# Four-byte pairs for the on-chip transposes, B and C loaded ahead of x, and a reordered head, in a state-space-plus-FFN kernel

## The chip, the cores and the metric

The kernel runs on one core of one Trainium2 chip. The metric is the device time of one execution in microseconds (us). Most executions agree within 1%; a few were marked slow (more than 1.5% above the fastest of the same kernel) and are left out of ratios. "Before" and "after" are the kernels without and with the change. A run's name, such as e5, is that of an experiment below.

The engines are TensorE (PE in the profile; PEld is its weight load), VectorE (DVE), ScalarE (ACT), GpSimd (POOL) and SyncE (SP), which only issues loads and stores here.

## The reference

The first half is a chunked linear-attention recurrence over 4 batches, 8 heads, 768 tokens; the second half is a gated FFN on 3072 tokens.

```python
# x: (4, 8, 768, 32)  a: (4, 8, 768)  B, C: (4, 8, 768, 16), all float32
cum = cumsum(log(a)) per chunk of 32
y   = (C B^T * exp(cum_i - cum_j) * causal) x  +  exp(cum) * (C state)
state = exp(cum_last) * state + sum_j exp(cum_last - cum_j) * B_j x_j
# then, with y as (3072, 256), w_gate and w_val (256, 1536), w_out (1536, 256):
out = (relu(y w_gate) * (y w_val)) w_out
```

The kernel multiplies C by running products of a (the tile `FC`) and B by their reciprocals (`FB`), so that the decay is inside the operands.

## The kernel before: the parts that matter

The FFN runs in six blocks of 512 tokens. B and C must be scaled and turned (state index onto partitions) once per batch. Batch b+1 is prepared inside FFN block b, for b = 0, 1, 2; blocks 3 to 5 have nothing to prepare. Batch 0 is prepared in the head, before the first block. A preparation has three steps.

```python
def scale(j, b, t, eng):                 # step 1: f32 -> bf16, times FB or FC
    eng.tensor_tensor(
        out=sq[j, b][:, :, t * N:(t + 1) * N],
        in0=rows[j, b][:, t].rearrange("p (k n) -> p k n", n=N),
        in1=(FB if j == "B" else FC)[:, 2 * b + t].to_broadcast([128, K, N]), op=ALU.mult)

def turn(j, b):                          # step 2: 32 x 32 transposes on VectorE
    tq[j, b] = glob.tile([128, K, R], BF16, ...)
    nc.vector.transpose(tq[j, b], sq[j, b])

def tidy_b(b, r0, r1, eng):              # step 3: tokens back in order
    dst = BT[b][:, K * r0:K * r1].rearrange("p (r k) -> p r k", k=K)
    (eng.copy ...)(out=dst, in_=tq["B", b][:, :, r0:r1].rearrange("p k r -> p r k"))
# tidy_c: the same for C, times a mask, into two halves
```

Here K is 24 tokens per row, R is 32 rows and N is 16 state columns. A tidy reads bf16 elements that lie 64 bytes apart. The main loop:

```python
for b in range(NBLK):
    for n in (P + 1, P + 2):                     # x of the next two pairs of chunks
        if n < NPAIR: load_x(n, nc.sync)
    if b in (1, 2):                              # B and C of the next batch
        for j, src in (("B", B), ("C", C)):
            rows[j, b + 1] = load_rows(src, b + 1, nc.sync, ...)
    def prep(step):
        if step < 2:   scale("B", n, step, nc.gpsimd); scale("C", n, step, nc.gpsimd)
        elif step < 4: turn("BC"[step - 2], n)
        elif step < 8: # 8 of the 32 rows per step
            tidy_b(.., nc.scalar); tidy_c(.., 0, nc.scalar); tidy_c(.., 1, nc.gpsimd)
    ...                                          # four 256-wide FFN steps, twice
    for f in range(4, NF):                       # eight 512-wide FFN steps
        if b == 0 and f == 4:
            factors(2, 8)                        # FC of batches 1 to 3
            for n in range(1, NB): inverse(n)    # FB of batches 1 to 3
        gv(b, f)                                 # gate, val, relu, product h
        prep(f - 4)
        ...                                      # cast_x on GpSimd, state matmuls A_ps
    ...                                          # fout: the output matmuls o
in_order(tc)                                     # each engine keeps the order of the program
```

Of the kernel before, what the change touches and what calls it, by code (L numbers as in the profile page):

```python
# [7 lines left out]

FP32 = mybir.dt.float32
BF16 = mybir.dt.bfloat16  # L10
AF = mybir.ActivationFunctionType
ALU = mybir.AluOpType

# [16 lines left out]
def kernel(  # L30
# [27 lines left out]

    const = ctx.enter_context(tc.tile_pool(name="const", bufs=1))
    glob = ctx.enter_context(tc.tile_pool(name="glob", bufs=1))  # L60
    raw = ctx.enter_context(tc.tile_pool(name="raw", bufs=4))
    att = ctx.enter_context(tc.tile_pool(name="att", bufs=3))
    ffn = ctx.enter_context(tc.tile_pool(name="ffn", bufs=2))
    mm = ctx.enter_context(tc.tile_pool(name="mm", bufs=1, space=bass.MemoryType.PSUM))
# [9 lines left out]
    def load_rows(src, b, q, name):  # L74
        rows = glob.tile([128, 2, K * N], FP32, name="%s%d" % (name, b))
        q.dma_start(out=rows, in_=src[b].rearrange("(t q) (r k) n -> (q r) t (k n)", t=2, r=R))
        return rows

    def load_x(p, *qs):
        b, c0 = p // PPB, 2 * (p % PPB)  # L80
        xr = raw.tile([128, 2, NH, D], FP32, tag="xr", name="xr")
        for i in range(2):
            sl = slice((c0 + i) * 128, (c0 + i + 1) * 128)
            qs[i % len(qs)].dma_start(out=xr[:, i], in_=x[b, :, sl, :].rearrange("h s d -> s h d"))  # L84
        st[p] = {"xr": xr}
# [2 lines left out]
    av = a.rearrange("b (t q) (r k) -> (q r) (b t) k", t=2, r=R)  # L88
    nc.sync.dma_start(out=al[:, 0:2, 1:], in_=av[:, 0:2])
    rows = {}  # L90
    rows["B", 0] = load_rows(B, 0, nc.scalar, "br")
    rows["C", 0] = load_rows(C, 0, nc.sync, "cr")
    load_x(0, nc.sync, nc.scalar)
    nc.sync.dma_start(out=al[:, 2:, 1:], in_=av[:, 2:])

    first = const.tile([1, 2], FP32)
# [28 lines left out]
    def keep_warm(n):  # L125
        w = bank("w")
        for _ in range(n):
            nc.tensor.matmul(out=w, lhsT=warm[:, 0:128], rhs=warm, start=True, stop=True)

    keep_warm(8)  # L130

    wg = glob.tile([128, 2, DF], BF16)
    wv = glob.tile([128, 2, DF], BF16)
# [2 lines left out]
    def weights(f0, f1):  # L136
        fs = slice(f0 * 128, f1 * 128)
        for w, src in ((wg, moe_w_gate), (wv, moe_w_val)):
            nc.gpsimd.dma_start(
                out=w[:, :, fs], in_=src[:, fs].rearrange("(k p) f -> p k f", k=2))  # L140
# [8 lines left out]
    def wait_for(j, cell):  # L149
        nc.gpsimd.tensor_copy(gate[:, j:j + 1], cell)  # L150
# [24 lines left out]
    def inverse(b):  # L175
        nc.vector.reciprocal(FB[:, 2 * b:2 * b + 2], FC[:, 2 * b:2 * b + 2])
# [5 lines left out]
    CT = [glob.tile([128, 2, S], BF16, name="CT%d" % b) for b in range(NB)]  # L182


    sq, tq = {}, {}

    def scale(j, b, t, eng):
        if (j, b) not in sq:
            sq[j, b] = glob.tile([128, K, 2 * N], BF16, name="sq%s%d" % (j, b))
        eng.tensor_tensor(  # L190
            out=sq[j, b][:, :, t * N:(t + 1) * N],
            in0=rows[j, b][:, t].rearrange("p (k n) -> p k n", n=N),
            in1=(FB if j == "B" else FC)[:, 2 * b + t].to_broadcast([128, K, N]), op=ALU.mult)

    def turn(j, b):
        tq[j, b] = glob.tile([128, K, R], BF16, name="tq%s%d" % (j, b))
        nc.vector.transpose(tq[j, b], sq[j, b])  # L197

    def span(i, b, r0, r1):
        return tq[i, b][:, :, r0:r1].rearrange("p k r -> p r k")  # L200

    def tidy_b(b, r0, r1, eng):
        dst = BT[b][:, K * r0:K * r1].rearrange("p (r k) -> p r k", k=K)
        (eng.copy if eng is nc.scalar else eng.tensor_copy)(out=dst, in_=span("B", b, r0, r1))  # L204

    def tidy_c(b, t, r0, r1, eng):
        dst = CT[b][:, t, K * r0:K * r1].rearrange("p (r k) -> p r k", k=K)
        if eng is nc.scalar:
            eng.mul(dst, span("C", b, r0, r1), tmask[:, t:t + 1])  # L209
        else:  # L210
            eng.tensor_scalar_mul(dst, span("C", b, r0, r1), tmask[:, t:t + 1])  # L211

    yT = glob.tile([128, 2, T], BF16)
    A_ps = mm.tile([128, 2, 128], FP32, tag="Aps", name="A_ps")
# [60 lines left out]
    def astep(p, i):  # L275

        c = 2 * (p % PPB) + i
        if c == NC - 1:
            return
        nc.tensor.matmul(  # L280
            out=A_ps, lhsT=st[p]["B"][i], rhs=st[p]["x"][i],
            start=(c == 0), stop=(c == NC - 2), skip_group_check=True)

    def sevac(p, i):
        if 2 * (p % PPB) + i == NC - 1:
            return
        S[2 * p + i + 1] = n = att.tile([128, 2, 128], BF16, tag="Sm", name="Sm", bufs=5)
        nc.vector.tensor_tensor(out=n, in0=A_ps, in1=smask, op=ALU.mult)

    def state(p, i):  # L290
        astep(p, i)
        sevac(p, i)
# [98 lines left out]


    factors(0, 2)
    inverse(0)
    wait_for(0, al[0:1, 0, 1:2])
    weights(0, 4)
    scale("B", 0, 0, nc.vector)
    scale("C", 0, 0, nc.gpsimd)
    scale("B", 0, 1, nc.vector)
    scale("C", 0, 1, nc.vector)  # L400
    load_x(1, nc.sync)
    turn("B", 0)
    tidy_b(0, 0, 11, nc.scalar)
    turn("C", 0)
    tidy_c(0, 0, 0, 11, nc.scalar)
    tidy_c(0, 1, 0, 11, nc.vector)
    cast_x(0, nc.scalar)
    keep_warm(10)
    rows_b(0)
    G(0)  # L410
    astep(0, 0)
    sevac(0, 0)
    gevac(0, half=False)
    wait_for(1, st[1]["xr"][0:1, 1, 0, 0:1])
    weights(4, 8)
    load_x(2, nc.sync)
    rows["B", 1] = load_rows(B, 1, nc.sync, "br")
    rows["C", 1] = load_rows(C, 1, nc.sync, "cr")
    keep_warm(4)
    Dm(0)  # L420
    inter(0, 1)
    astep(0, 1)
    yevac(0, nc.scalar)
    tidy_b(0, 11, R, nc.scalar)
    tidy_c(0, 0, 11, R, nc.scalar)
    tidy_c(0, 1, 11, R, nc.gpsimd)
    rows_b(1)
    cast_x(1, nc.scalar)
    sevac(0, 1)

    for b in range(NBLK):
        P, Q, W = 2 * b + 2, 2 * b + 3, 2 * b + 1
        more = P < NPAIR
        for n in (P + 1, P + 2):
            if n < NPAIR:
                load_x(n, nc.sync)
        if b in (1, 2):
            for j, src in (("B", B), ("C", C)):
                rows[j, b + 1] = load_rows(src, b + 1, nc.sync, j.lower() + "r")

        def at(name, *fs):

            return more and f == fs[min(b, len(fs) - 1)]

        def prep(step):
            n = b + 1
            if n >= NB:
                return
            if step < 2:
                scale("B", n, step, nc.gpsimd)  # L450
                scale("C", n, step, nc.gpsimd)
            elif step < 4:
                turn("BC"[step - 2], n)
            elif step < 8:
                r = 8 * (step - 4)
                tidy_b(n, r, r + 8, nc.scalar)
                tidy_c(n, 0, r, r + 8, nc.scalar)
                tidy_c(n, 1, r, r + 8, nc.gpsimd)

        for f in range(4):  # L460
            gvh(b, f, 0)
            if b == 0 and f == 0:
                G(1)
                gevac(1)
                state(1, 0)
                weights(8, NF)
                wait_for(2, st[2]["xr"][0:1, 1, 0, 0:1])
                weights_out(0, NF)
            if f == (3 if b == 0 else 1):
                if b == 1:  # L470
                    state(W, 1)
                inter(W, 0)
                inter(W, 1)
                Dm(W)
                if b == 0:
                    state(1, 1)
                yevac(W, nc.scalar)
        for f in range(4):
            gvh(b, f, 1)
        for f in range(4, NF):  # L480
            if b == 0 and f == 4:
                factors(2, 8)
                for n in range(1, NB):
                    inverse(n)
            gv(b, f)
            if f in (4, 5):
                prep(f - 4)
            if f >= 6:
                prep(f - 4)
            if at("cast P", 6, 4, 4):  # L490
                cast_x(P, nc.gpsimd)
            if at("cast Q", 8, 5, 4):
                cast_x(Q, nc.gpsimd)
            if at("rows P", 7, 6, 5):
                rows_b(P)
            if at("state P0", 9, 8, 7):
                state(P, 0)
            if at("state P1", 10, 10, 9):
                state(P, 1)
            if at("rows Q", 99, 9, 8):  # L500
                rows_b(Q)
        if more:
            inter(P, 0)
            inter(P, 1)
        fout(b, 0)
        foevac(b, 0)
        if more:
            G(P)
            gevac(P)
        if b == 0:  # L510
            rows_b(Q)
        fout(b, 1)
        foevac(b, 1)
        if more and b > 0:
            state(Q, 0)
        fout(b, 2)
        foevac(b, 2)
        if more:
            Dm(P)
            yevac(P, nc.scalar)  # L520
            G(Q)
            gevac(Q)
            state(Q, 1 if b else 0)
        fout(b, 3)
        foevac(b, 3)
# [32 lines left out]
```

## Time and profile before

| | before |
|---|---|
| median of 3 runs | 150.23 us (149.98 to 150.93) |
| span of the profiled run | 147.2 us |
| head (to the first gate matmul of block 0) | 14.92 us |
| blocks 0, 1, 2 (start to start) | 25.56, 24.50, 26.24 us |
| blocks 3, 4 | 18.24, 18.12 us |
| block 5 with the last store | 19.62 us |
| mean granted TensorE clock | 0.954 |

A block starts here with its first `gv` matmul in the trace. Blocks 0 to 2 differ from 3 and 4 by about 6 to 8 us each, and the preparation is the work that only they have.

The table of stretches of before, from a block's start to its first output matmul (blocks 1, 2, 3); a row has the stretch, its length, busy time of each engine with the number of instructions, granted clock, DMA share, and GB/s:

```profile
core 0: us, PE busy (x) PEld busy (x) DVE busy (x) ACT busy (x) POOL busy (x), PEclk, DMA share, GB/s
...
40.48:57.06 16.58, 12.40 (x93) 7.48 (x92) 10.44 (x21) 10.33 (x23) 7.23 (x11) 0.98 0.41 95
...
64.98:83.06 18.08, 13.53 (x94) 7.69 (x93) 10.06 (x20) 10.18 (x23) 7.21 (x11) 0.91 0.38 88
...
91.22:102.79 11.57, 11.52 (x93) 7.22 (x92) 9.12 (x19) 9.20 (x20) 1.67 (x4) 1.00 0.37 70
```

In block 3 TensorE is busy for 11.52 of 11.57 us: it is the limit. In blocks 1 and 2 it does the same matmuls with gaps of 4.2 and 4.6 us, and no other engine is full. I read that as the latency of a chain, not a lack of rate; e1 and e8 bear it out. The timeline of block 1 of before shows the chain (start, duration, engine, line, operation, output and inputs, and in brackets how long the engine sat idle and what ended it; xN is the number of merged instructions):

```profile
41.77 2.83 SPq L84 DMA_DIRECT2D xr<-in_x_dram  x4
...
44.65 0.67 SPq L76 DMA_DIRECT2D br<-in_B_dram  x1
...
45.36 0.47 SPq L76 DMA_DIRECT2D cr<-in_C_dram  x1
...
48.95 0.84 POOL L190 TENSOR_TENSOR sqB<-br,FB 128x384 bf16<-128x384 f32 x1 [7.98 <-DMA br<-in_B_dram]
49.95 0.84 POOL L190 TENSOR_TENSOR sqC<-cr,FC 128x384 bf16<-128x384 f32 x1 [0.16 <-DMA cr<-in_C_dram]
50.73 0.61 POOL L219 CAST xb<-xr 128x512 bf16<-128x512 f32 x1
51.30 0.83 POOL L190 TENSOR_TENSOR sqB<-br,FB 128x384 bf16<-128x384 f32 x1
51.39 0.27 PE L280 MATMUL A_ps<-xb,bt 128*128 128x256 bf16 x1 [2.16 <-POOL xb L219]
...
52.17 0.98 DVE L197 STREAM_TRANSPOSE tqB<-sqB 128x768 bf16<-128x768 bf16 x1 [3.86 <-POOL sqB L190]
...
53.65 0.96 DVE L197 STREAM_TRANSPOSE tqC<-sqC 128x768 bf16<-128x768 bf16 x1
```

SyncE issues four x loads first, so B is issued 2.9 us after the queue is free. GpSimd waits 7.98 us for it. Because every engine keeps its order, the x cast stands behind the scales, TensorE's state matmul behind the cast, and VectorE's products behind the transpose.

The costs of the three steps, from the groups of before with shapes kept apart (line, engine, operation, count; total busy us, mean ns of one; idle before and what ended it):

```profile
L209 ACT ACTIVATE CT<-tqC,tmask 128x192 bf16<-128x192 bf16 x12 | 7.5, 626 | 2.8 <-DVE tqC L197 2.8
...
L204 ACT COPY BT<-tqB 128x192 bf16<-128x192 bf16 x12 | 6.2, 516 | 5.3 <-DVE tqB L197 5.3
...
L190 POOL TENSOR_TENSOR sqB<-br,FB 128x384 bf16<-128x384 f32 x6 | 5.0, 837 | 20.0 <-DMA br<-in_B_dram 15.5 <-DVE FB L176 4.5
...
L197 DVE STREAM_TRANSPOSE tqB<-sqB 128x768 bf16<-128x768 bf16 x4 | 3.9, 975 | 9.4 <-POOL sqB L190 9.4
...
L190 DVE TENSOR_TENSOR sqC<-cr,FC 128x384 bf16<-128x384 f32 x1 | 1.2, 1212 | 0.0
...
L190 DVE TENSOR_TENSOR sqB<-br,FB 128x384 bf16<-128x384 f32 x2 | 1.0, 554 | 0.0
```

The scales on VectorE are those of the head. Two took 0.55 us; the third ran beside a scale on GpSimd and took 1.21 us.

### The profile page before, as it was taken

To read this page: it belongs to the slowest core of one execution; us is meant where nothing else is said; L and a number is where in the kernel's file an instruction comes from. 1 tells how busy PE (TensorE), PEld (TensorE's weight loads), DVE (VectorE), ACT (ScalarE), POOL (GpSimd) and SP (SyncE) were. 2 spreads that over 40 slices of the span, in tenths; PEclk is the share of its full clock that TensorE was granted. 3 is DMA by queue.
4 is the path that set the end of the run, shared out by engine and by line. 5 is a ranking of instruction groups with operands and counts; after the bars stand their busy time and mean duration, and the time that the engine had idled before them with its cause. 6 is when DMAs were issued, how large, how long until landed. Compare 5 with 4: busy or idle time off the path is not lost.

```text
span 147.2 us, 2902 instructions
## 1 busy us (share of the span) xinstructions
PE 124.8 (85%) x1056; PEld 79.2 (54%) x1062; DVE 94.1 (64%) x201; ACT 89.2 (61%) x188; POOL 48.5 (33%) x78
## 2 busy tenths in 40 slices
PE   6945989677999459999709979999999999999991
PEld 2312564235785126677303557845777458774580
DVE  6964479975478185647607665778657786477711
ACT  4084856478588329568603975877359763687520
POOL 5509561975210668220155923010230102200000
PEclk9996599999999996899995999999999999999999
DMA  4999999900259200028900002640026000220022
GB/s 129 231 204 253 200 159 154 128 0 2 76 119 213 97 0 0 4 71 172 253 6 0 0 0 71 144 76 0 2 76 142 0 4 0 71 76 0 0 71 71
DMA packets 34685, 12.07 MB, mean 82 GB/s; under 512 B 26480, under 2 KB 34672, under 8 KB 34672
## 3 DMA queue, kind: packets, MB, share of 16 engines
q1 hardware_dynamic: 29888, 8.75, 26.3%
q0 software_dynamic: 3184, 2.36, 11.6%
q10 hardware_dynamic: 1600, 0.79, 2.0%
q8 instruction: 8, 0.13, 0.4%
q14 instruction: 5, 0.04, 0.1%
HBM read 11.11 MB, written 3.15 MB: 97 GB/s over the span
## 4 chain that ended last, share of the span: by engine, by line
PE 56%; DVE 10%; ACT 8%; DMA 7%; issue 7%; POOL 6%; SPq 4%; POOLq 0%; DVEq 0%; ACTq 0%
PE o L372 20%; PE gv L360 10%; PE val L345 8%; PE gate L342 8%; DMA br<-in_B_dram 6%; SPq L84 4%; POOL sqB L190 3%; PE g L244 3%; PE y L317 3%; DVE tqC L197 2%; ACT BT L204 2%; PE A_ps L280 2%; POOL xb L219 2%; ACT r L348 2%; ACT CT L209 1%
## 5 line engine op out<-in xcount | busy, mean ns | idle before, releaser
L349 DVE TENSOR_TENSOR h<-r,val 128x512 bf16<-128x512 bf16 x48 | 32.5, 681 | 10.3 <-ACT r L348 10.3
L372 PE MATMUL o<-wo,h 128*128 128x256 bf16 x288 | 36.4, 279 | 2.2 <-DVE h L349 2.1
L348 ACT ACTIVATE r<-gate 128x512 bf16<-128x512 f32 x48 | 28.6, 597 | 14.1 <-PE gate L342 12.2
L372 PEld LDWEIGHTS <-h 128*128 128x128 bf16 x288 | 28.0, 100 | 8.2 <-DVE h L349 3.3
L345 PE MATMUL val<-yT,wv 128*128 128x512 bf16 x96 | 29.3, 388 | 1.3 <-DVE h L349 0.8
L342 PE MATMUL gate<-yT,wg 128*128 128x512 bf16 x90 | 28.2, 390 | 0.6 <-DVE h L349 0.6
L364 DVE TENSOR_TENSOR h<-r,gv 128x256 bf16<-128x256 bf16 x48 | 19.9, 421 | 9.9 <-ACT r L363 9.5
L251 POOL TENSOR_SCALAR_AFFINE_SELECT gs<-gs 128x512 bf16<-128x512 bf16 (+1 forms) x24 | 12.2, 532 | 42.6 <-ACT gs L262 42.6
L268 DVE TENSOR_TENSOR gs<-g,maskUT 128x512 bf16<-128x512 f32 x24 | 15.4, 685 | 12.7 <-PE g L244 9.6
L363 ACT ACTIVATE r<-gv 128x256 bf16<-128x256 f32 x48 | 18.5, 385 | 3.1 <-PE gv L360 1.7
L360 PE MATMUL gv<-yT,wg 128*128 128x256 bf16 x96 | 19.4, 285 | 0.5 <-ACT yT L330 0.5
L360 PE MATMUL gv<-yT,wv 128*128 128x256 bf16 x96 | 19.1, 282 | 0.0
L342 PEld LDWEIGHTS <-wg 128*128 128x128 bf16 x96 | 9.2, 99 | 17.5 <-issue 10.5
L345 PEld LDWEIGHTS <-wv 128*128 128x128 bf16 x96 | 9.6, 100 | 13.5 <-issue 2.9
L211 POOL TENSOR_SCALAR CT<-tqC,tmask 128x192 bf16<-128x192 bf16 (+1 forms) x13 | 13.0, 1010 | 4.2 <-DVE tqC L197 4.2
L204 ACT COPY BT<-tqB 128x192 bf16<-128x192 bf16 (+2 forms) x14 | 7.9, 562 | 9.7 <-DVE tqB L197 9.7
L280 PE MATMUL A_ps<-xb,bt 128*128 128x256 bf16 x20 | 5.8, 292 | 8.8 <-POOL xb L219 6.8
L330 ACT CAST yT<-y 128x512 bf16<-128x512 f32 x12 | 7.0, 586 | 8.9 <-PE y L317 6.8
L190 POOL TENSOR_TENSOR sqB<-br,FB 128x384 bf16<-128x384 f32 x6 | 5.0, 837 | 20.0 <-DMA br<-in_B_dram 15.5
L209 ACT ACTIVATE CT<-tqC,tmask 128x192 bf16<-128x192 bf16 (+2 forms) x14 | 9.4, 672 | 3.0 <-DVE tqC L197 3.0
L360 PEld LDWEIGHTS <-wv 128*128 128x128 bf16 x96 | 9.8, 102 | 1.5
L360 PEld LDWEIGHTS <-wg 128*128 128x128 bf16 x96 | 9.3, 102 | 2.4 <-issue 0.6
(62 smaller groups left out, 115.4 us busy)
## 6 DMA issues: line engine op xcount, KB each, us to landing
xr<-in_x_dram SPq DMA_DIRECT2D x23, 128.0 KB, 3.6
out_dram<-ob SPq DMA_DIRECT2D x10, 256.0 KB, 2.2
cr<-in_C_dram SPq DMA_DIRECT2D x4, 384.0 KB, 4.7
br<-in_B_dram SPq DMA_DIRECT2D x3, 384.0 KB, 4.2
wg<-in_moe_w_gate_dram POOLq DMA_DIRECT2D x3, 256.0 KB, 5.3
wv<-in_moe_w_val_dram POOLq DMA_DIRECT2D x3, 256.0 KB, 6.3
wo<-in_moe_w_out_dram POOLq DMA_DIRECT2D x1, 768.0 KB, 9.9
br<-in_B_dram ACTq DMA_DIRECT2D x1, 384.0 KB, 3.3
```

Of the source, the lines that this page charges most:

```text
L209: eng.mul(dst, span("C", b, r0, r1), tmask[:, t:t + 1])
L211: eng.tensor_scalar_mul(dst, span("C", b, r0, r1), tmask[:, t:t + 1])
L251: nc.gpsimd.affine_select(out=dst, in_=dst, pattern=[[0, n], [1, 128]], compare_op=ALU.is_ge, fill=0.0, base=0, channel_multiplier=-1)
L268: nc.vector.tensor_tensor(out=d[:, q], in0=g[q], in1=m, op=ALU.mult)
L342: nc.tensor.matmul(out=g, lhsT=wg[:, k, fs], rhs=yT[:, k, tk], start=(k == 0), stop=(k == 1))
L345: nc.tensor.matmul(out=v, lhsT=wv[:, k, fs], rhs=yT[:, k, tk], start=(k == 0), stop=(k == 1))
L348: nc.scalar.activation(r, g, AF.Relu)
L349: nc.vector.tensor_tensor(out=fst[b][:, f], in0=r, in1=v, op=ALU.mult)
L360: nc.tensor.matmul(out=gv_[:, j], lhsT=w[:, k, fs], rhs=yT[:, k, tk], start=(k == 0), stop=(k == 1), skip_group_check=True)
L363: nc.scalar.activation(r, gv_[:, 0], AF.Relu)
L364: nc.vector.tensor_tensor(out=fst[b][:, f, u * 256:(u + 1) * 256], in0=r, in1=gv_[:, 1], op=ALU.mult)
L372: nc.tensor.matmul(out=o[:, ts % 2], lhsT=fst[b][:, f, ts * 128:(ts + 1) * 128], rhs=wo[:, f], start=(f == 0), stop=(f == NF - 1), skip_gr ...
```

## The change

The intent: transpose pairs of neighbouring tokens as one 4-byte element, which halves the elements of a transpose and lets a tidy read two elements at each stop; get the loads out of the way; let the head prepare C first. The price is that the scale now reads its f32 input in pairs 64 bytes apart.

```diff
     def scale(j, b, t, eng):
+        f = (FB if j == "B" else FC)[:, 2 * b + t].rearrange("p (a k) -> p a k", k=2)
         eng.tensor_tensor(
-            out=sq[j, b][:, :, t * N:(t + 1) * N],
-            in0=rows[j, b][:, t].rearrange("p (k n) -> p k n", n=N),
-            in1=(FB if j == "B" else FC)[:, 2 * b + t].to_broadcast([128, K, N]), op=ALU.mult)
+            out=sq[j, b][:, :, t * N:(t + 1) * N, :],
+            in0=rows[j, b][:, t].rearrange("p (a k n) -> p a n k", n=N, k=2),
+            in1=f.unsqueeze(2).to_broadcast([128, KK, N, 2]), op=ALU.mult)      # KK = 12
     def turn(j, b):
-        nc.vector.transpose(tq[j, b], sq[j, b])
+        nc.vector.transpose(tq[j, b]...bitcast(U32), sq[j, b]...bitcast(U32))
     # tidies: "p a r k -> p r a k", that is 4 contiguous bytes at each stop
 # head: C loaded, scaled and turned first, then B; x(0), x(1) on one queue; 13 warm-up
 #   matmuls instead of 18; second part of the tidies spread over VectorE and ScalarE;
 #   G(1) and rows_b(1) before block 0                                          (cut)
 for b in range(NBLK):
+        if b < 3:
+            for j, src in (("B", B), ("C", C)):
+                rows[j, b + 1] = load_rows(src, b + 1, nc.sync, j.lower() + "r")
         for n in (P + 1, P + 2):
             if n < NPAIR:
                 load_x(n, nc.sync)
-        if b in (1, 2):
-            ... rows[j, b + 1] = load_rows(...)
         def prep(step):
+            if step == 0:
+                inverse(n)                     # one reciprocal per block, on VectorE
             ...
-            elif step < 8:                     # 8 rows per step
+            elif step < 7:                     # 11 rows per step
         ...
             if b == 0 and f == 4:
                 factors(2, 8)
-                for n in range(1, NB): inverse(n)
```

The x tiles also get one buffer per pair instead of four in all. In the head all four scales now run on VectorE, where before one ran on GpSimd.

More of the change, by code (lines that the diff above doesn't have):

```diff
@@ L10 @@
 BF16 = mybir.dt.bfloat16
+U32 = mybir.dt.uint32
 AF = mybir.ActivationFunctionType
@@ L60 @@
     glob = ctx.enter_context(tc.tile_pool(name="glob", bufs=1))
-    raw = ctx.enter_context(tc.tile_pool(name="raw", bufs=4))
+    raw = ctx.enter_context(tc.tile_pool(name="raw", bufs=NPAIR))
     att = ctx.enter_context(tc.tile_pool(name="att", bufs=3))
@@ L77, in load_rows, with load_x @@
         return rows
-    def load_x(p, *qs):
+    def load_x(p, *qs, after=None):
         b, c0 = p // PPB, 2 * (p % PPB)
         xr = raw.tile([128, 2, NH, D], FP32, tag="xr", name="xr")
+        if after is not None:
+            after.memset(xr[0:1, :, 0, 0:1], 0.0)
         for i in range(2):
@@ L90 @@
     rows = {}
-    rows["B", 0] = load_rows(B, 0, nc.scalar, "br")
-    rows["C", 0] = load_rows(C, 0, nc.sync, "cr")
-    load_x(0, nc.sync, nc.scalar)
+    rows["C", 0] = load_rows(C, 0, nc.scalar, "cr")
+    rows["B", 0] = load_rows(B, 0, nc.sync, "br")
+    load_x(0, nc.sync)
+    load_x(1, nc.sync)
     nc.sync.dma_start(out=al[:, 2:, 1:], in_=av[:, 2:])
@@ L128, in keep_warm @@
             nc.tensor.matmul(out=w, lhsT=warm[:, 0:128], rhs=warm, start=True, stop=True)
-    keep_warm(8)
+    keep_warm(13)
     wg = glob.tile([128, 2, DF], BF16)
@@ L182 @@
     CT = [glob.tile([128, 2, S], BF16, name="CT%d" % b) for b in range(NB)]
+    KK = K // 2
     sq, tq = {}, {}
@@ L188, in scale @@
         if (j, b) not in sq:
-            sq[j, b] = glob.tile([128, K, 2 * N], BF16, name="sq%s%d" % (j, b))
+            sq[j, b] = glob.tile([128, KK, 2 * N, 2], BF16, name="sq%s%d" % (j, b))
+        f = (FB if j == "B" else FC)[:, 2 * b + t].rearrange("p (a k) -> p a k", k=2)
         eng.tensor_tensor(
-            out=sq[j, b][:, :, t * N:(t + 1) * N],
-            in0=rows[j, b][:, t].rearrange("p (k n) -> p k n", n=N),
-            in1=(FB if j == "B" else FC)[:, 2 * b + t].to_broadcast([128, K, N]), op=ALU.mult)
+            out=sq[j, b][:, :, t * N:(t + 1) * N, :],
+            in0=rows[j, b][:, t].rearrange("p (a k n) -> p a n k", n=N, k=2),
+            in1=f.unsqueeze(2).to_broadcast([128, KK, N, 2]), op=ALU.mult)
@@ L195, in turn @@
     def turn(j, b):
-        tq[j, b] = glob.tile([128, K, R], BF16, name="tq%s%d" % (j, b))
-        nc.vector.transpose(tq[j, b], sq[j, b])
-    def span(i, b, r0, r1):
-        return tq[i, b][:, :, r0:r1].rearrange("p k r -> p r k")
+        tq[j, b] = glob.tile([128, KK, R, 2], BF16, name="tq%s%d" % (j, b))
+        nc.vector.transpose(
+            tq[j, b].rearrange("p a r k -> p (a r k)").bitcast(U32),
+            sq[j, b].rearrange("p a n k -> p (a n k)").bitcast(U32))
     def tidy_b(b, r0, r1, eng):
-        dst = BT[b][:, K * r0:K * r1].rearrange("p (r k) -> p r k", k=K)
-        (eng.copy if eng is nc.scalar else eng.tensor_copy)(out=dst, in_=span("B", b, r0, r1))
+        dst = BT[b][:, K * r0:K * r1]
@@ L206, in tidy_c @@
+        src = tq["B", b][:, :, r0:r1, :]
+        if eng is nc.scalar:
+            eng.copy(out=dst.rearrange("p (r a k) -> p r a k", a=KK, k=2),
+                     in_=src.rearrange("p a r k -> p r a k"))
+        else:
+            eng.tensor_copy(
+                dst.bitcast(U32).rearrange("p (r a) -> p r a", a=KK),
+                tq["B", b].rearrange("p a r k -> p (a r k)").bitcast(U32)
+                .rearrange("p (a r) -> p r a", r=R)[:, r0:r1])
     def tidy_c(b, t, r0, r1, eng):
-        dst = CT[b][:, t, K * r0:K * r1].rearrange("p (r k) -> p r k", k=K)
+        dst = CT[b][:, t, K * r0:K * r1].rearrange("p (r a k) -> p r a k", a=KK, k=2)
@@ L208, in tidy_c @@
+        src = tq["C", b][:, :, r0:r1, :].rearrange("p a r k -> p r a k")
         if eng is nc.scalar:
-            eng.mul(dst, span("C", b, r0, r1), tmask[:, t:t + 1])
+            eng.mul(dst, src, tmask[:, t:t + 1])
         else:
-            eng.tensor_scalar_mul(dst, span("C", b, r0, r1), tmask[:, t:t + 1])
+            eng.tensor_scalar_mul(dst, src, tmask[:, t:t + 1])
     yT = glob.tile([128, 2, T], BF16)
@@ L393 @@
     factors(0, 2)
-    inverse(0)
-    wait_for(0, al[0:1, 0, 1:2])
+    nc.vector.reciprocal(FB[:, 0:2], FC[:, 0:2])
+    scale("C", 0, 0, nc.vector)
+    scale("C", 0, 1, nc.vector)
+    turn("C", 0)
+    wait_for(0, rows["B", 0][0:1, 0, 0:1])
     weights(0, 4)
+    tidy_c(0, 0, 0, 11, nc.scalar)
     scale("B", 0, 0, nc.vector)
-    scale("C", 0, 0, nc.gpsimd)
     scale("B", 0, 1, nc.vector)
-    scale("C", 0, 1, nc.vector)
-    load_x(1, nc.sync)
     turn("B", 0)
-    tidy_b(0, 0, 11, nc.scalar)
-    turn("C", 0)
-    tidy_c(0, 0, 0, 11, nc.scalar)
-    tidy_c(0, 1, 0, 11, nc.vector)
+    tidy_c(0, 1, 0, 11, nc.scalar)
+    tidy_b(0, 0, 11, nc.vector)
     cast_x(0, nc.scalar)
-    keep_warm(10)
     rows_b(0)
@@ L411 @@
     astep(0, 0)
+    gevac(0, half=False)
+    tidy_b(0, 11, R, nc.vector)
     sevac(0, 0)
-    gevac(0, half=False)
+    tidy_c(0, 0, 11, R, nc.scalar)
+    tidy_c(0, 1, 11, R, nc.vector)
     wait_for(1, st[1]["xr"][0:1, 1, 0, 0:1])
     weights(4, 8)
-    load_x(2, nc.sync)
-    rows["B", 1] = load_rows(B, 1, nc.sync, "br")
-    rows["C", 1] = load_rows(C, 1, nc.sync, "cr")
+    load_x(2, nc.sync, after=nc.gpsimd)
     keep_warm(4)
@@ L423 @@
     yevac(0, nc.scalar)
-    tidy_b(0, 11, R, nc.scalar)
-    tidy_c(0, 0, 11, R, nc.scalar)
-    tidy_c(0, 1, 11, R, nc.gpsimd)
+    sevac(0, 1)
     rows_b(1)
-    cast_x(1, nc.scalar)
-    sevac(0, 1)
+    G(1)
     for b in range(NBLK):
@@ L436 @@
                 load_x(n, nc.sync)
-        if b in (1, 2):
-            for j, src in (("B", B), ("C", C)):
-                rows[j, b + 1] = load_rows(src, b + 1, nc.sync, j.lower() + "r")
         def at(name, *fs):
@@ L453, in prep @@
                 turn("BC"[step - 2], n)
-            elif step < 8:
-                r = 8 * (step - 4)
-                tidy_b(n, r, r + 8, nc.scalar)
-                tidy_c(n, 0, r, r + 8, nc.scalar)
-                tidy_c(n, 1, r, r + 8, nc.gpsimd)
+            elif step < 7:
+                r = 11 * (step - 4)
+                r1 = min(r + 11, R)
+                tidy_b(n, r, r1, nc.scalar)
+                tidy_c(n, 0, r, r1, nc.scalar)
+                tidy_c(n, 1, r, r1, nc.gpsimd)
         for f in range(4):
@@ L462 @@
             if b == 0 and f == 0:
-                G(1)
                 gevac(1)
+            if b == 0 and f == 1:
+                cast_x(1, nc.scalar)
                 state(1, 0)
@@ L482 @@
                 factors(2, 8)
-                for n in range(1, NB):
-                    inverse(n)
             gv(b, f)
```

## The prediction

> **What bounds the kernel now.** Profiled span 147.2 us. The chain of waits and the timeline give six FFN blocks. From 91 us on a block takes 18.2 us and TensorE is 99% busy in it (table of stretches). The first three take 25.7 (14.8 to 40.5), 24.5 and 26.1 us, 21.7 us above that pace, after a head of 14.8 us. So some 22 us are lost while B and C of the *next* batch are prepared inside a block. Blocks 1 and 2: the SyncE queue frees at 41.8, issues four x loads (2.9 us), then B, then C; GpSimd waits for B until 48.95 (73.1 in block 2), then runs four scales of 0.84 us with the x casts between. The state matmul waits for a cast (2.2 and 4.1 us idle), VectorE for the B transpose (3.9 and 5.4 us), and from the end of the C transpose (54.6) 5.3 us of tidies, relu and products pass before the first output group ends. Block 0 has no load wait (scales start at 25.4, after the factors) but the same chain, at a low clock (0.72 at 15 to 22 us).
>
> **Costs.**
> - Transposes: 768 elements take 0.96 us; 384 four-byte ones about 0.57 us [...]. None of this size is in the trace.
> - Tidies on ScalarE: 192 elements at 64-byte stride take 0.52 (B) and 0.63 us (C), 1.7 ns per element, against 0.83 contiguous. [...] I expect 0.41 and 0.50 us for 264: 2.7 us per batch instead of 4.6.
> - GpSimd tidies: 0.93 us for 192; about 0.9 for 264.
> - The bill: scales now read f32 at 64-byte stride. [...] I estimate 0.95 us per scale (now 0.55) in the head, and 1.2 us (0.84 to 1.5) on GpSimd.
> - Loads: B and C go before x and land 2.9 us earlier. But the reciprocal now sits behind the first 512-wide product, so the scales start at about 47.0 in block 1 (1.9 us earlier), and 0.6 us later in block 0.
>
> **On the critical path.** Head: slower scales nearly eat the shorter transposes, but the second part of the tidies no longer delays the first gate matmul: gain 0.5 to 1.5 us. Block 0: -1 to +1. Block 1: 1.9 from the load, 0.4 from the transpose, less 1.4 from scales: 1 to 3. Block 2: 2 to 4. Shorter tidies after the C transpose, 0.2 per block; fewer low-clock matmuls, 0.5. Blocks 3 to 5: nothing. Sum about 5 us: predicted 145.0 us, range 139.0 to 149.5. Faster by over 2%: 0.64; within 2%: 0.24; slower: 0.12.
>
> **What would show it.** Groups: tq transpose near 0.57; ScalarE BT copies of 264 near 0.41, CT near 0.50; GpSimd scale near 1.2, VectorE scale near 0.95. Waits: GpSimd no longer waits for B beyond about 47.0 and 71.5, but for the reciprocal; the state matmul waits under 2 us for the cast in block 2. Timeline: first gate matmul at 13.5 to 14.5; block 3 onward 18.2 us each.
>
> **What would make it wrong.** Scales not slowed by the stride: about 139 us. GpSimd scales at 1.6 us or more, half-rate 4-byte transposes, or pairs no faster on ScalarE: 148 to 151. First weights, now behind B's landing, arriving after yT. A clock that falls elsewhere in the head.

The sum: about 5 us (its terms come to 7.1, see "Why the prediction was wrong"). These figures are estimates; what the trace of before gives for them is this:

- Transposes, 0.57 us: 32 four-byte elements took 0.21 to 0.24 us (L163, L170) and 768 two-byte ones 0.95 to 0.98 us (L197). On a straight line between the two, 384 elements take 0.58 us. That the time goes with the number of elements, whatever their bytes, was not shown before the run.
- Tidies, 0.41 and 0.50 us: ScalarE took 516 ns for 192 elements at a 64-byte step and 637 ns for 264 (L204), 1.7 ns for each; its contiguous relus took 385 ns for 256 elements and 597 ns for 512 (L363, L348), 0.83 ns for each. With 0.83 ns in place of 1.7 and the rest of a tidy's time as it was, 264 elements come to 0.41 us for B and 0.52 for C. That pairs go at the contiguous pace was an assumption.
- Tidies on GpSimd, about 0.9 us: before took 0.93 us for 192 elements at a 64-byte step and 1.99 us for 504 (L211), 3.4 ns for each. At this pace 264 come to 1.17 us, at half of it per element to 0.72; 0.9 lies between. After took 0.96.
- Scales on VectorE, 0.95 us: its one strided tidy took 669 ns for 264 elements (L211 on DVE), and at the same time per element 384 come to 0.97 us. That this carries over to the scale was an assumption.
- Scales on GpSimd, 1.2 us: the middle of the range from 0.84 us (measured, no charge) to about 1.45 us (0.84 x 0.95 / 0.55, the whole of VectorE's charge).
- Clock, 0.5 us: a part of TensorE's extra busy time where the clock of before was lower. The same matmuls kept TensorE busy for 12.40 and 13.53 us in the stretches of blocks 1 and 2, at clocks of 0.98 and 0.91, and for 11.52 us in block 3 at 1.00, so up to 2.9 us in these two blocks.

## The result

| | before | after |
|---|---|---|
| median of 3 runs | 150.23 us | 139.35 us (138.68 to 139.39) |
| span of the profiled run | 147.2 us | 137.4 us |
| head | 14.92 us | 13.81 us |
| blocks 0, 1, 2 | 25.56, 24.50, 26.24 us | 24.64, 21.10, 21.88 us |
| blocks 3, 4 | 18.24, 18.12 us | 18.23, 18.12 us |
| block 5 with the last store | 19.62 us | 19.62 us |
| mean granted TensorE clock | 0.954 | 0.984 |

The ratio is 0.9253, 95% interval 0.9189 to 0.9317. A ratio here is the mean time of one kernel's fast runs over that of the other's in the same rounds, so it is not quite the ratio of the medians. In a repeat on another chip (run e0) after took 139.37 us and before 149.21 us, ratio 0.9341. The two measurements of after thus differ by 0.0088, or 1.3 us, and a comparison across batches can be wrong by as much.

The direction was right and the size was wrong: 5.2 us were forecast and 10.9 us came. All the gain is where it was looked for, in the head and in blocks 0 to 2.

The table of stretches of after, the same parts of the same three blocks:

```profile
core 0: us, PE busy (x) PEld busy (x) DVE busy (x) ACT busy (x) POOL busy (x), PEclk, DMA share, GB/s
...
38.45:51.94 13.49, 12.15 (x95) 7.27 (x93) 9.86 (x22) 9.94 (x23) 7.24 (x11) 1.00 0.54 117
...
59.55:73.76 14.21, 11.94 (x94) 7.22 (x92) 9.56 (x21) 10.08 (x23) 7.33 (x11) 1.00 0.52 112
...
81.43:92.99 11.56, 11.56 (x94) 7.20 (x92) 9.12 (x19) 9.20 (x20) 1.67 (x4) 1.00 0.37 70
```

The gaps of TensorE in blocks 1 and 2 fell from 4.2 and 4.6 to 1.3 and 2.3 us, and the clock is 1.00 in both. Not only the gaps fell: in block 2 the same matmuls kept TensorE busy for 13.53 us at a clock of 0.91 before, and for 11.94 us at 1.00 after. No run separates the clock from the gaps. The timeline of block 1 of after:

```profile
39.69 0.46 SPq L77 DMA_DIRECT2D br<-in_B_dram  x1
...
40.21 0.49 SPq L77 DMA_DIRECT2D cr<-in_C_dram  x1
...
40.74 4.14 SPq L87 DMA_DIRECT2D xr<-in_x_dram  x4
...
44.47 0.44 DVE L180 RECIPROCAL FB<-FC 128x48 f32<-128x48 f32 x1
...
45.00 0.88 POOL L197 TENSOR_TENSOR sqB<-br,FB 128x384 bf16<-128x384 f32 x1 [5.88 <-DVE FB L180]
...
45.84 0.88 POOL L197 TENSOR_TENSOR sqC<-cr,FC 128x384 bf16<-128x384 f32 x1
...
46.67 0.61 POOL L234 CAST xb<-xr 128x512 bf16<-128x512 f32 x1
...
47.33 0.27 PE L295 MATMUL A_ps<-xb,bt 128*128 128x256 bf16 x1
...
48.15 0.58 DVE L204 STREAM_TRANSPOSE tqB<-sqB 128x384 uint32<-128x384 uint32 x1 [1.87 <-POOL sqB L197]
```

B is issued first, and GpSimd no longer waits for B but for the reciprocal. It starts 6.55 us after the block's start (45.00 - 38.45), against 8.47 us before (48.95 - 40.48). The groups of after:

```profile
L197 POOL TENSOR_TENSOR sqB<-br,FB 128x384 bf16<-128x384 f32 x6 | 5.3, 879 | 15.7 <-DVE FB L180 15.7
...
L224 ACT ACTIVATE CT<-tqC,tmask 128x264 bf16<-128x264 bf16 x8 | 4.1, 528 | 6.5 <-DVE tqC L204 6.5
...
L212 ACT COPY BT<-tqB 128x264 bf16<-128x264 bf16 x6 | 2.5, 414 | 4.1 <-DVE tqB L204 4.1
...
L204 DVE STREAM_TRANSPOSE tqB<-sqB 128x384 uint32<-128x384 uint32 x4 | 2.3, 578 | 5.8 <-POOL sqB L197 5.8
...
L197 DVE TENSOR_TENSOR sqB<-br,FB 128x384 bf16<-128x384 f32 x2 | 1.0, 534 | 0.0
L197 DVE TENSOR_TENSOR sqC<-cr,FC 128x384 bf16<-128x384 f32 x2 | 1.0, 522 | 0.0
```

The transpose (578 ns) and the tidies of 264 elements (414 and 528 ns) came out as forecast (570, 410, 500 ns). The scales did not. I had charged 1.2 us on GpSimd and 0.95 us on VectorE, and they take 0.88 and 0.53 us (0.84 and 0.55 before): almost nothing for the stride.

### The profile page after: what moved, and what is told of

The parts are those of the page before. It is cut to its first block, busy times and chain, and to the rows that moved or that the text cites. A ratio compares the mean times of both kernels' runs of the same rounds, so it can differ in the third digit from the quotient of the medians.

```text
span 137.4 us, 2883 instructions
## 1 busy us (share of the span) xinstructions
PE 119.8 (87%) x1057; PEld 76.8 (56%) x1057; DVE 91.5 (67%) x204; ACT 83.2 (61%) x181; POOL 43.5 (32%) x74
## 4 chain that ended last, share of the span: by engine, by line
PE 55%; DVE 11%; ACT 9%; DMA 9%; POOL 6%; issue 5%; SPq 2%; DVEq 0%; POOLq 0%; ACTq 0%
PE o L387 20%; PE gv L375 9%; PE val L360 8%; PE gate L357 8%; DMA xr<-in_x_dram 3%; POOL sqB L197 3%; PE g L259 3%; DMA br<-in_B_dram 3%; PE y L332 3%; DVE h L364 3%; DMA al<-in_a_dram 2%; ACT r L363 2%; ACT CT L224 2%; POOL xb L234 2%; PE A_ps L295 2%
## 5 line engine op out<-in xcount | busy, mean ns | idle before, releaser
L387 PE MATMUL o<-wo,h 128*128 128x256 bf16 x288 | 35.1, 273 | 2.3 <-DVE h L364 2.3
L363 ACT ACTIVATE r<-gate 128x512 bf16<-128x512 f32 x48 | 28.6, 596 | 9.8 <-PE gate L357 8.6
L387 PEld LDWEIGHTS <-h 128*128 128x128 bf16 x288 | 27.4, 98 | 7.6 <-DVE h L364 3.0
L360 PE MATMUL val<-yT,wv 128*128 128x512 bf16 x96 | 28.6, 379 | 0.8 <-DMA wv<-in_moe_w_val_dram 0.4
L375 PE MATMUL gv<-yT,wg 128*128 128x256 bf16 x96 | 18.4, 273 | 0.5 <-ACT yT L345 0.5
L375 PE MATMUL gv<-yT,wv 128*128 128x256 bf16 x96 | 18.3, 273 | 0.0
L357 PEld LDWEIGHTS <-wg 128*128 128x128 bf16 x96 | 9.0, 98 | 13.5 <-issue 6.5
L360 PEld LDWEIGHTS <-wv 128*128 128x128 bf16 x96 | 9.3, 98 | 12.6 <-DMA wv<-in_moe_w_val_dram 0.9
L277 ACT CAST gs<-g 128x512 bf16<-128x512 f32 x12 | 7.0, 587 | 8.0 <-PE g L259 7.9
L375 PEld LDWEIGHTS <-wg 128*128 128x128 bf16 x96 | 8.9, 98 | 4.0 <-issue 2.6
L224 ACT ACTIVATE CT<-tqC,tmask 128x264 bf16<-128x264 bf16 (+2 forms) x12 | 6.4, 542 | 6.5 <-DVE tqC L204 6.5
L197 POOL TENSOR_TENSOR sqB<-br,FB 128x384 bf16<-128x384 f32 x6 | 5.3, 879 | 15.7 <-DVE FB L180 15.7
L375 PEld LDWEIGHTS <-wv 128*128 128x128 bf16 x96 | 9.4, 98 | 1.1
L234 POOL CAST xb<-xr 128x512 bf16<-128x512 f32 x10 | 6.1, 612 | 8.9 <-DMA xr<-in_x_dram 4.9
```

Of the source, the lines that this page charges most:

```text
L197: eng.tensor_tensor(out=sq[j, b][:, :, t * N:(t + 1) * N, :], in0=rows[j, b][:, t].rearrange("p (a k n) -> p a n k", n=N, k=2), in1=f.unsq ...
L224: eng.mul(dst, src, tmask[:, t:t + 1])
L357: nc.tensor.matmul(out=g, lhsT=wg[:, k, fs], rhs=yT[:, k, tk], start=(k == 0), stop=(k == 1))
L360: nc.tensor.matmul(out=v, lhsT=wv[:, k, fs], rhs=yT[:, k, tk], start=(k == 0), stop=(k == 1))
L363: nc.scalar.activation(r, g, AF.Relu)
L375: nc.tensor.matmul(out=gv_[:, j], lhsT=w[:, k, fs], rhs=yT[:, k, tk], start=(k == 0), stop=(k == 1), skip_group_check=True)
```

## The experiments

All kernels gave correct results. Each batch was timed against before on its own chip, so runs of different batches are compared by their ratios to before. A difference of 0.01 in the ratio is 1.5 us.

My theory (A): the charge for the scales' stride is what is missing from the forecast. Rivals: the load order is worth much more than I put (B), or the scales had slack and the rest came from elsewhere (C).

### e1: the loads alone

In before, `load_rows` for blocks 1 and 2 moved ahead of the x loads; nothing else.

```diff
+        if b in (1, 2): ... rows[j, b + 1] = load_rows(...)
         for n in (P + 1, P + 2): ... load_x(n, nc.sync)
-        if b in (1, 2): ... rows[j, b + 1] = load_rows(...)
```

> The kernel before with one edit: in blocks 1 and 2 the B and C loads are issued before the four x loads (the factors' reciprocals stay where they were, all done in block 0). Theory A (the scales' stride cost that I charged is what is missing; the load order is worth about what I put, 2 to 3.5 us per block): GpSimd's first scale starts at about 45.5 instead of 48.95 in block 1 and 70 instead of 73.1 in block 2, and the time is 143 to 146 us. Rival B (the loads are nearly the whole gain, and worth twice what I put): 139 to 142 us.

Measured: 142.39 us, ratio 0.9516 (0.9453 to 0.9579). Blocks 1 and 2 took 22.06 and 22.38 us, 2.4 and 3.9 us less than before. GpSimd's first scale of block 1 started 5.78 us after the block's start instead of 8.47. The load order alone brings 7.2 us (0.0484 of 149.25), and the median lies between the two ranges that I had given. So it is worth more than theory A allowed, although rival B, which would leave nothing for the pairs, fails at e2. In the profiles the two blocks gain 6.3 us together and block 0 loses 0.6.

### e2: the pairs alone

The new `scale`, `turn` and tidies put into before; order of loads, head, reciprocals and four tidy steps as before.

```diff
-    (scale, turn, tidy_b, tidy_c of before)
+    (scale, turn, tidy_b, tidy_c of after)
```

> The kernel before with the 4-byte pairs alone (scales, transposes, tidies in the new layout; order of loads, head and reciprocals as before). Theory A: scales 0.88 us on GpSimd and 0.53 on VectorE as in the kernel after, so only gains remain: transposes 0.4 us on the chain of each of three blocks, tidies 0.2 to 0.3 each, about 1 us in the head: 146.5 to 148.5 us. Rival B (loads are nearly all): within 1 us of the kernel before. My forecast's own numbers (scales of 1.2 and 0.95 us) would give about 152 us.

Measured: 143.85 us, ratio 0.9605 (0.9528 to 0.9681), 5.9 us. The head became 12.72 us (2.2 less), block 1 23.02 and block 2 24.40 us (1.5 and 1.8 less); block 0 did not change. GpSimd's scales took 0.88 us. This is below the range that I gave for theory A: I had put too little on the pairs, in the two blocks and in the head, where all three steps stand in one line with nothing beside them. Some 0.5 us of the head's gain is not the pairs': with the same head, e8 took 13.27 us. In before and e8 the VectorE scale that overlaps a GpSimd scale took 1.21 and 1.23 us.

### e3: the scales' charge imposed by dummy work

After, with a memset of a scratch tile in front of every scale on the same engine.

```diff
+        eng.memset(pad_v if eng is nc.vector else pad_p, 0.0)
         eng.tensor_tensor(out=sq[j, b]...
```

> The kernel after with a dummy memset in front of each scale on the same engine (400 f32 elements on VectorE, 300 on GpSimd), meant to add what I had forecast for the stride: some 0.4 us per scale on VectorE in the head, 0.3 to 0.4 us on GpSimd. Theory A: these lie on the chain in full; with 4 x 0.35 in each of three blocks and 4 x 0.4 in the head the time goes to 143.5 to 145.5 us, my forecast. Rival C (the scales had slack, the missing gain came from elsewhere): at most 141 us.

Measured: 142.47 us, ratio 0.9538 (0.9493 to 0.9584). That is 0.0197 above e0, or 2.9 us. From one GpSimd scale to the next the start moved from 0.84 to about 1.13 us, so a dummy added about 0.3 us. The result lies between the two expectations. One reason can be read in the trace: the first dummy of blocks 1 and 2 ran while GpSimd was waiting for the reciprocal anyway, so from the start of the first scale to the end of the fourth 4.83 us passed instead of 3.96, three dummies and not four. Blocks 1 and 2 grew by 0.65 and 0.63 us against the profile of e0, block 0 by 0.6 and the head, where the four dummies of VectorE stand, by 1.7. The dummies are an imperfect copy of a slow scale, which is why e5 was the better test.

### e5: the scales really made slow, by the order of their walk

After, with the scale walking all 24 tokens of one state column before it goes on to the next. Same data, same result, same number of elements.

```diff
-            in0=rows[j, b][:, t].rearrange("p (a k n) -> p a n k", n=N, k=2),
+            in0=rows[j, b][:, t].rearrange("p (a k n) -> p n a k", n=N, k=2),
```

(`out` and `in1` are turned in the same way, so the writes change too: in after they come in runs of 32 neighbouring elements, in e5 each pair of bf16 lies 128 bytes from the one before it.) In after the reads go to and fro between two places 64 bytes apart, and both move on by 4 bytes each time. In e5 each of 24 reads in a row lies 64 bytes from the one before it. Theory D says that the scale of after is not slowed because it comes back near the same two places, and that the walk of e5 slows it; rival E says that the order does not matter.

> The kernel after with the scales' walk turned: all 24 tokens of one state column, then the next column[...]; same data, same result. [...] Theory D [...]: VectorE scale 0.9 to 1.0 us, GpSimd scale 1.2 us or more, time 142 to 146 us. Rival E [...]: 0.53 and 0.88 us, time as the kernel after.

Measured: 143.15 us, ratio 0.9582 (0.9533 to 0.9631). The groups of e5:

```profile
L197 POOL TENSOR_TENSOR sqB<-br,FB 128x384 bf16<-128x384 f32 x6 | 7.1, 1183 | 15.0 <-DVE FB L180 15.0
L197 POOL TENSOR_TENSOR sqC<-cr,FC 128x384 bf16<-128x384 f32 x6 | 7.1, 1176 | 0.0
...
L197 DVE TENSOR_TENSOR sqB<-br,FB 128x384 bf16<-128x384 f32 x2 | 1.5, 778 | 0.0
...
L197 DVE TENSOR_TENSOR sqC<-cr,FC 128x384 bf16<-128x384 f32 x2 | 1.4, 745 | 0.0
```

GpSimd's scale now takes 1.18 us, just what I had forecast for after, and VectorE's 0.75 to 0.78 us, about half of the extra that I had forecast. Rival E, no penalty at all, falls. Theory D fits the time and, but for 0.02 us, GpSimd; VectorE's 0.75 to 0.78 us is less than the 0.9 to 1.0 that it asked for. That the order of the reads is the reason is not shown, since the writes were reordered with them. The kernel is 0.0241 of before slower than e0, or 3.6 us (4.9 us against the first measurement of after, which was in another batch too). So a kernel that has nearly the scales that I forecast gains 6.2 us over before, close to my 5.2, and after without them gains 9.8. The profile of e5 agrees stage by stage: against before the head gained 0.9 us, block 0 lost 0.6, and blocks 1 and 2 gained 2.4 and 3.4; the midpoints of my forecast were 1, 0, 2 and 3, with 1.1 us for tidies and clock not shared out. After gained 1.1, 0.9, 3.4 and 4.4.

### e0 and e4: after again, and after with x loaded first

e0 is after unchanged, so that a batch of its own could be compared. e4 puts the x loads back in front of B and C in blocks 1 and 2.

> The kernel after, unchanged, so that the next three can be compared on one chip; 138 to 140 us. It also shows whether the factors' own load, which landed at 4.12 us in the first profile of after against 2.87 in before, is late in every execution (then the new order of the head costs about 1 us) or only in that one.

> The kernel after with the x loads put back before B and C in blocks 1 and 2. If the loads are worth what they were worth alone (6.9 us, run e1), 144.5 to 146.5 us; if pairs and loads overlap, that is if the order is worth less once the chain behind it is shorter or waits for the reciprocal, 142 to 144 us.

Measured: e0 139.37 us, ratio 0.9341 (0.9280 to 0.9402), head 13.17 us. The factors' load was used at 3.50 us in e0 and between 3.43 and 3.48 us in the profiles of e3, e4, e5 and e6, which have the same head, but at 4.14 us in the first profile of after, and at 2.89 us in before. The first profile was thus a late one by 0.6 us. Some lateness remains in the new head, about 0.5 us (3.02 us in e8, which has the old head), and I have no cause for it.

e4: 143.14 us, ratio 0.9607 (0.9545 to 0.9669). Inside after the load order is worth 4.0 us (0.0266), against 7.2 us alone. The next two runs show why: in after the scales wait for the reciprocal anyway (e6), and with the pairs but with early reciprocals the order is worth 7.1 us (e8 against e2).

### e6: the reciprocals back in block 0

After, with one edit: all three reciprocals right after the factors, as in before.

```diff
-            if step == 0:
-                inverse(n)
 ...
                 factors(2, 8)
+                for n in range(1, NB):
+                    inverse(n)
```

> The kernel after with all three reciprocals in block 0 again, as in the kernel before. In after GpSimd waits for the reciprocal until 45.0 and 66.1 us while B had landed at 43.4 and about 64.7. Theory F (the late reciprocal holds blocks 1 and 2): 1 to 1.5 us shorter each, less 0.7 us of VectorE work added to block 0: 136.5 to 138.5 us. Rival G (GpSimd's start is no longer what ends last, as half of the padding of run e3 was already hidden): within 0.7 us of after.

Measured: 136.91 us, ratio 0.9185 (0.9132 to 0.9239), 2.3 us faster than e0 (0.0156). The timeline of block 1 of e6:

```profile
38.66 0.46 SPq L77 DMA_DIRECT2D br<-in_B_dram  x1
...
42.32 0.88 POOL L197 TENSOR_TENSOR sqB<-br,FB 128x384 bf16<-128x384 f32 x1 [4.22 <-DMA br<-in_B_dram]
```

GpSimd starts 4.91 us after the block's start (42.32 - 37.41) and waits for B again. In after it started at 6.55. Blocks 1 and 2 shrank from 21.10 and 21.89 us in e0 to 19.86 and 21.38, and block 0, which got two more reciprocals, from 24.69 to 24.32. A second profile of e6 shows how much such figures scatter: its first scale of block 1 starts 5.33 us after the block, and blocks 0 to 2 take 24.87, 20.30 and 21.45 us. Theory F holds. The late reciprocal was a part of the change that took back part of what the load order gave.

### e8: pairs and loads, nothing else of the change

The edits of e1 and e2 together, on before.

> The kernel before with the 4-byte pairs and the early B and C loads, but the head, the reciprocals, the four tidy steps and the four x buffers of before. If the two parts add up (6.9 and 5.4 us): 136.5 to 137.5 us, faster than after, and what else the change did costs 1 to 2 us. If after's other parts help: 139.5 us or more.

Measured: 135.96 us, ratio 0.9129 (0.9055 to 0.9202), the fastest of these and 0.0212 (3.2 us) below after. The two parts add up: 5.9 + 7.2 = 13.1 us, measured 13.0 us. From e2 to e8 the first scale moved forward by 3.6 us within block 1 and within block 2, and each became 3.4 us shorter: the earlier scales are enough to account for it. So the rest of the change costs 3.2 us net. The late reciprocals are 2.3 of them; the remaining 0.8 us (new head, three tidy steps, buffers) is within the intervals of e6 and e8, which overlap. The spans of the two profiled runs are both 134.6 us. The head took 13.27 us in e8 and 13.09 us in e6. Profiles of the new head lie between 12.63 and 13.81 us (after, e0, e4, e6), so no gain of turning C first is shown once both have the pairs.

### e11 and e12: which of the pairs' savings counts

e8 with a dummy VectorE memset before each transpose, and e8 with a dummy ScalarE copy before each pair of tidies.

```diff
+        nc.vector.memset(pad_v, 0.0)                       # e11
         nc.vector.transpose(...)
+            eng.copy(out=pad_a, in_=warm[:, 0:256])        # e12
             eng.copy(out=dst..., in_=src...)
```

> Run e8 (pairs and loads) with a dummy VectorE memset of 520 f32 elements before each of the eight large transposes, about 0.4 us each, which gives back what the 4-byte transposes save. If the transposes are the larger part of what the pairs bring: 3 us slower than e8 or more. If they are on the chain once per block and twice in the head (0.4 us each): 1.5 to 2 us slower. If hidden: under 0.7 us.

> Run e8 with a dummy ScalarE copy of 256 contiguous elements before each pair of tidies on ScalarE, 0.3 us or a little more each, which gives back what the pairs save in a pair of tidies (0.52 + 0.63 - 0.36 - 0.47 us). If ScalarE's tidies with the relus between them are the tail of the chain in blocks 0 to 2: 0.8 to 1.2 us per block and 0.5 in the head, 2.5 to 4 us slower than e8. If hidden: under 1 us.

Measured: e11 139.39 us, ratio 0.9341, which is 0.0212 or 3.2 us above e8. e12 138.05 us, ratio 0.9250, 0.0121 or 1.8 us above e8. A dummy moved a transpose by 0.41 us (its own record is 0.49). In the profiles e11 lost 1.1 us in the head, 0.7 in block 1 and 1.7 in block 2; e12 lost 0.3, 0.8 and 0.7. So both savings of the pairs lie on the chain, and the transposes seem the larger part. For e12 that is less than I expected. As in e3 not every dummy counts: in e11 those before the B transposes of blocks 1 and 2 ran while VectorE waited for the scale (it sat idle for another 0.39 and 1.36 us), and in e12 the first of block 1 moved its tidy by only 0.2 us. A dummy of e12 took 0.40 us, against the 0.31 that a pair of tidies saves. Block 0 lost nothing in either run. Together they give back 5.0 us of the 5.9 that the pairs bring alone, so the split is rough; GpSimd's tidies, also shorter with the pairs (four of 192 elements took 3.02 us in block 1 of e2, 3.66 in e1), were not padded.

### e9 and e10: further along the same line

e9 is e6 with B and C of batch b+2 loaded in block b, so that they have landed when block b+1 starts; GpSimd scales at once in blocks 1 and 2, the transposes and tidies come two steps earlier, and the head's second x cast goes to GpSimd. e10 also moves block 0's factors and scales forward.

```diff
+        if b < 2: ... rows[j, b + 2] = load_rows(src, b + 2, ...)      # after the x loads
         for f in range(4):
             gvh(b, f, 0)
+            if b > 0 and f < 2: prep(f)
 ...
-            prep(f - 4)
+            prep(f - 4) if b == 0 else prep(f - 2)
```

> Run e6 (reciprocals early) with B and C of batch b+2 loaded during block b, so that in blocks 1 and 2 GpSimd scales at once at the start of the block and the transposes and tidies move two steps forward; the second x cast of the head goes to GpSimd. If the load's landing and the scales behind it are what still keeps blocks 1 and 2 above 18.2 us (19.9 and 21.4 in e6), both come to 18.5 to 19 us and the time to 132.5 to 134.5 us. If ScalarE's load (relu and tidies) bounds them, less than 1 us of gain.

> Run e9 with, in block 0 too, the factors, one reciprocal and the scales moved forward (factors before the second half of the 256-wide products; B and C of batch 1 loaded before the x tile of pair 2). If block 0 (24.3 us) is held by the late factors as blocks 1 and 2 were by the late loads, 1 to 2.5 us faster than e9. If its length comes from the loads of the weights and the cold start, or the factors only move VectorE's work in front of the products, the same as e9 or slower.

Measured: e9 133.71 us, ratio 0.8983 (0.8947 to 0.9018). Blocks 1 and 2 took 19.10 and 19.15 us. They were a little longer than expected, and the time was in the range. This is the best kernel, faster than both before and after.

e10: 135.53 us, ratio 0.9078, slower than e9. Its block 0 took 25.59 instead of 24.33 us. It doesn't test its theory: the reciprocal of batch 1 ended near 21.3 us, but GpSimd was held in its own order by a wait for the x tile of pair 2 (3.88 us, to 22.1) and an issue of weights, and scaled only at 23.26 us. The run is inconclusive on what holds block 0. The "cold start" of its expectation is a supposition: what the traces show is a granted clock of 0.72 from 15 to 22 us in before, and of 1.00 over block 0 of after.

## Why the prediction was wrong, point by point

- **Where the time was lost: right.** Blocks 3, 4 and 5 did not move (18.2, 18.1 and 19.6 us in both), and the gain is in the head and blocks 0 to 2.
- **Transposes near 0.57, tidies near 0.41 and 0.50 us: right** (0.578, 0.414, 0.528). The transpose of 128x768 bf16 as 128x384 uint32 took 0.578 us instead of 0.975: 384 elements fewer save 397 ns, 1.03 ns for each. The one ScalarE copy of 264 elements in before took 637 ns at a 64-byte step, and the copies of after, in 4-byte pairs, 414 ns. What sets these times is not shown. e11 and e12 show that both savings count.
- **When GpSimd can start: right.** I put the first scale of block 1 at about 47.0 us on before's clock, 6.5 us after that block's start at 40.48; it was 6.55. That it would then wait for the reciprocal was also right. I did not see that this made the change worse than its two main parts; e6 measured it at 2.3 us.
- **First gate matmul at 13.5 to 14.5 us: right** (13.81; 13.17 in e0). The state matmul's wait for the cast in block 2 was 1.00 us, under 2 as said.
- **The step that failed: "the bill: scales now read f32 at 64-byte stride", 0.95 us on VectorE and 1.2 us on GpSimd.** They took 0.53 and 0.88. I carried the factor two of the bf16 tidies (1.7 against 0.83 ns per element on ScalarE) over to the scales because both have 64-byte steps. But a tidy goes on by 64 bytes with every element, and the scale goes to and fro between two places that move on by 4 bytes. Put in another order, writes included (e5), the scales took 1.18 us on GpSimd and 0.75 to 0.78 on VectorE, and the kernel lost 3.6 us. So a penalty of this size exists and lies on the chain, but the access pattern of the change does not pay it. VectorE's part would have been too large even if it did. Whether the reads or the writes of e5 pay it stays open.
- **The sum was added up wrongly.** My stages had midpoints of 1, 0, 2 and 3 us, with 0.6 for tidies and 0.5 for the clock. That is 7.1 us, and I wrote "about 5" and 145.0, which is 5.2 below before. The 1.9 us lost there and the 3.6 us of the scales make 5.5 us, near the gap of 5.7 us between 5.2 and 10.9. That they come so close is luck: the 3.6 us are taken from e0, against which the gap is only 4.6 us, and against the first measurement of after they would be 4.9 (a ratio is good to about 0.006, or 0.9 us).
- **The case "scales not slowed by the stride: about 139 us"** was in the text and is what happened. It was treated as an edge of the range instead of being checked against the order in which the addresses are visited, which the diff shows.
- **Two sizes that partly cancel.** The load order alone was worth 7.2 us (e1) and the pairs alone 5.9 (e2), both more than I would have said; the other edits took 3.2 back (e8).

What stays open: why the factors' load lands 0.5 us later in the new head; what block 0's remaining 6 us are made of; how the 0.8 us beside the reciprocals split, or whether they are there at all; how much the clock did; whether e5 is slow by its reads or by its writes.

## What to carry to other kernels

Before charging an access pattern for its stride, write down the addresses that it touches in order: here steps of 64 bytes to and fro between two places cost 5% on GpSimd (0.84 to 0.88 us) and nothing on VectorE (0.55 to 0.53 us), and the same elements in an order that goes on by 64 bytes each time, with the writes spread as well, cost 41% on GpSimd (1.18 us), and 0.75 to 0.78 us on VectorE. When a change has several parts, run the two main parts alone and together; here that showed a version 3 us faster than the whole change, and one small part (a reciprocal moved next to its use, on an engine that keeps its order) that took 2.3 us back. And add up your own stages once more before writing the total.
